# Between the two phases of an attention and mixture-of-experts kernel: the order of the fetches, and which operand the early expert's last block keeps in the array

## The chip, the cores and the metric

One NeuronCore of one Trainium2 chip. The metric is the time of one execution in device microseconds; the time of the kernel before is the median of three runs, 576.55 us (576.1 to 577.07). The profile shows one execution of its own.

## The reference

Linear attention over 8 batches and 8 heads of 576 tokens, with a normalisation, gives 4608 rows of 512 features. Each row is then routed to one of 16 experts (a group of four first, then an expert in it) and goes through that expert's two matrices.

```
kv  = einsum('bhsd,bhse->bhde', k, v)
out = einsum('bhsd,bhde->bhse', q, kv)
x   = out / sqrt(mean(out*out, -1) + 1e-6) * g_norm      # rows of 8*64 = 512
g   = argmax(x @ w_group)                                # 4 groups
e   = argmax(x[rows of g] @ w_expert[g])                 # 4 experts in each
y[rows of g, e] = g_w * e_w * (relu(x @ w1[g, e]) @ w2[g, e])   # 512 -> 1024 -> 512
```

## The kernel before

**Two phases.** The first computes the attention, writes its rows to a table `scr` in HBM, counts the rows of each expert, and, once one expert (the early expert) is known, starts on it: 256 of its rows go through both of its matrices in plain fp32 (`l` in the rows of the profile, lines 299 and 303). What is left of that expert is done at the border: a last quarter of the second layer for these 256 rows (`st["h"]`, `w2c[1]`) and a third block of 128 rows that has yet to be gathered (`xr`, index column `gidx[:, 0, 2:3]`). The second phase is a loop over 15 regions, one expert each, with 364 rows in region 1 down to 256 in the last.

**A region** multiplies in split precision: weights and rows are split in a rounded part and a rest (`whi`, `wlo`, `xh`, `xl`, `hh`, `hl`), and three matmuls stand for one (L310, L311, L315). `split_piece` cuts weights by the piece: a cast on ScalarE (L245) and a subtraction on VectorE (L246). Layer 1 runs over eight feature blocks f, each with 12 matmuls in one of three PSUM buffers `ps`, that ScalarE (`hh`, L284) and then VectorE (`hl`, L285) read out. Layer 2 runs over four blocks in the buffers `psy`.

**Rows for a region** take a long way: an indirect gather from `scr` on GpSimd's queue (`gather`, L252), a scaling (`scale_rows`, L280), a write to HBM (`put_x`, `xd`, L1242), a read back in quarters (`get_x`, `xq`, L1248), a 32x32 transpose on VectorE (`xt`, L1253), and the split (L1262 on ScalarE, L1263 on VectorE).

**What sets the order around the change.** Every engine runs what the program gives it in the order in which the code was written; nothing overtakes on a queue. SyncE (SP) issues the weight loads (`load_half`, L212), `put_x`, `get_x`; GpSimd (POOL) issues gathers (L252) and scatters of finished rows (`scatter_rows`, L256). Weights, their split parts and the early expert's `st["ys"]` (finished rows, `yos`) live in one pool `big` of 12 buffers, used in rotation: a new tile waits until the last reader of its buffer is done, and for `yos` the last readers are two scatters.

At the border, SP's second half load was tied to the gathers by hand:

```
for i in range(2):
    load_next(i, st["gather"] if i else None)
```

and the border's 128 rows kept their rows in the array, so that the result came out by rows and had to be turned:

```
whole1(ps, xT, w1c[hf])        # stationary: 128 rows of xT; moving: 512 columns of weights
nc.scalar.activation(out=hr[:, hf * 512:(hf + 1) * 512], in_=ps, func=AF.Relu)
turn(0); turn(1)               # 8 transposes on TensorE, 2 copies on VectorE
```

The last quarter of the second layer ran in a `psy` buffer, in two parts (`CUT`), with the transposes of `xs` between them; the `psy` buffers were cleared first (L1338). Of the four pieces of region 1's first weights two were split at the border and two in region 1's layer 1 (`w1_at`).

Of the kernel before, what the change touches and what calls it, by code (L numbers as in the profile page):

```python
# [9 lines left out]
F32 = mybir.dt.float32  # L10
# [3 lines left out]
AF = mybir.ActivationFunctionType  # L14
# [40 lines left out]
CUT = 5  # L55

@with_exitstack
def tile_linattn_moe(ctx: ExitStack, tc: tile.TileContext, qm, qt, k, v, router, w1, w2, out):
    nc = tc.nc
    P = 128  # L60
    B, H, S, D = BATCH, HEADS, SEQ, HEAD_DIM
    NTOK, DM = out.shape
# [15 lines left out]
    FC = FF // P  # L78
# [172 lines left out]
    def gather_rows(xg, rows, idx, src=scr):  # L251
        return nc.gpsimd.indirect_dma_start(out=xg[0:rows, 0:RW], out_offset=None, in_=src,  # L252
                                            in_offset=bass.IndirectOffsetOnAxis(ap=idx[0:rows, :], axis=0))

    def scatter_rows(yo, rows, idx):
        sc = nc.gpsimd.indirect_dma_start(  # L256
            out=out, out_offset=bass.IndirectOffsetOnAxis(ap=idx[0:rows, :], axis=0), in_=yo[0:rows, :],
            in_offset=None, bounds_check=NTOK - 1, oob_is_err=False)
        tc.declare_no_dep(sc.ins, group=osc, reason="each token has a row of its own")
        tc.add_to_no_dep_group(osc, sc.ins)  # L260
# [13 lines left out]
    def scale_rows(eng, xg, out_=None):  # L274

        x = by_quarter(xg[:, 0:DM])
        out_ = x if out_ is None else by_chunk(out_)
        for h in range(2):
            hs = slice(2 * h, 2 * h + 2)
            d = eng.tensor_tensor(out=out_[:, hs], in0=x[:, hs], in1=factors(xg)[:, h], op=ALU.mult)  # L280
        return d
# [19 lines left out]
    def whole2(ps, h, w, lo=0, hi=FC):  # L301
        for c in range(lo, hi):
            nc.tensor.matmul(ps, lhsT=h[:, c, :], rhs=w[:, c, :], start=(c == 0), stop=(c == FC - 1))
# [833 lines left out]
    with ExitStack() as ph:  # L1137
# [81 lines left out]
        def next_psy():  # L1219
            psys.append(psys.pop(0))  # L1220
            return psys[-1]
# [8 lines left out]
        def gather(r):  # L1230
            xg = mp.tile([P, 3, RW], F32, name="xg", bufs=1)
            for j, _ in blocks(CAPS[r]):
                st["gather"] = gather_rows(xg[:, j], P, gidx[:, r, j:j + 1])
            return xg
# [5 lines left out]
        def put_x(r, g):  # L1240
            for j, rows in blocks(CAPS[r] + -CAPS[r] % 32):
                nc.sync.dma_start(xd[r % 2][j * P:j * P + rows, :], g[0:rows, j, 0:DM])  # L1242

        def get_x(r):
            n = (CAPS[r] + 31) // 32
            xq = mp.tile([P, 12, P], F32, name="xq", bufs=1)
            for a in range(4):
                nc.sync.dma_start(xq[32 * a:32 * a + 32, 0:n, :], quarter_rows(xd[r % 2], CAPS[r], a))  # L1248
            return xq, mp.tile([P, KC, 384], F32, name="xt", bufs=1)
# [74 lines left out]

        w1c, w2c = st["ws"][0:2], st["ws"][2:4]
        xT = mp.tile([P, KC, P], F32, name="xT", bufs=1)
        hr = mp.tile([P, 12, P], F32, name="hr", tag="yq", bufs=1).rearrange("p c t -> p (c t)")
        xr, xs = (mp.tile([P, 3 * DM], F32, name=nm, tag="yo3")[:, 0:n] for nm, n in (("xr", RW), ("xs", DM)))
        gather_rows(xr, P, gidx[:, 0, 2:3])
        nxt = gather(1)  # L1330
        w1n, w2n, load_next = weight_loads(eidx[0:1, 1:2], mp)
        for i in range(2):
            load_next(i, st["gather"] if i else None)
        scale_rows(nc.vector, xr, xs)
        for j, _ in blocks(CAPS[1]):
            scale_rows(nc.vector, nxt[:, j])
        for x in psys:
            nc.vector.memset(x[:, DM // 2:384], 0.0)  # L1338
        put_x(1, nxt)
        xq, xt = get_x(1)  # L1340
        for i in range(2, 4):
            load_next(i)
        nxt = gather(2)
        scale(2, nxt)
        ps = next_psy()
        o, h1 = ps[:, 0:DM // 2], st["h"]["h"][:, :, P:2 * P]
        whole2(o, h1, w2c[1], hi=CUT)
        tp = ps_t.tile([P, 512], F32, name="tp", tag="pst")
        for c in range(KC):
            nc.tensor.transpose(tp[:, c * P:(c + 1) * P], xs[:, c * P:(c + 1) * P], ident)  # L1350
        nc.scalar.activation(out=xT, in_=tp.rearrange("p (c t) -> p c t", c=KC), func=AF.Copy, scale=g2[:, 0:1])
        whole2(o, h1, w2c[1], lo=CUT)
        nc.scalar.copy(out=st["ys"][:, 1, DM // 2:DM], in_=o)
        for j in range(2):
            scatter_rows(st["ys"][:, j, :], P, gidx0[:, j:j + 1])
        hT = mp.tile([P, FC, 384], F32, name="hT", tag="hl", bufs=1)[:, :, 0:P]

        def turn(hf):
            tp = ps_h.tile([P, 512], F32, name="ps")
            for f in range(4):  # L1360
                nc.tensor.transpose(tp[:, f * P:(f + 1) * P], hr[:, (4 * hf + f) * P:(4 * hf + f + 1) * P], ident)
            nc.vector.tensor_copy(out=hT[:, 4 * hf:4 * hf + 4, :], in_=tp.rearrange("p (f t) -> p f t", f=4))

        for hf in range(2):
            split_piece(w1n, hf)
            ps = ps_h.tile([P, 512], F32, name="ps")
            whole1(ps, xT, w1c[hf])
            nc.scalar.activation(out=hr[:, hf * 512:(hf + 1) * 512], in_=ps, func=AF.Relu)
        turn(0)
        turn(1)  # L1370
        cur = parts_x()
        for c in range(KC):
            turn_x(1, xq, xt, c)
            split_x(1, cur, xt, c)
        yo = mp.tile([P, DM], F32, name="yo", bufs=2)
        for hf in range(2):
            ps = next_psy()
            o = ps[:, 0:DM // 2]
            whole2(o, hT, w2c[hf])
            nc.scalar.copy(out=yo[:, hf * (DM // 2):(hf + 1) * (DM // 2)], in_=o)  # L1380
# [3 lines left out]
        nw1, nw2, load_next = weight_loads(eidx[0:1, 2:3], None)  # L1384
        for i in range(2):
            load_next(i)
        w1_at = {0: 2, 1: 3}
        w2_at = {2: 0, 4: 1, 5: 2, 7: 3}
        todo, results, turns = None, [], iter(())
        tables = overflow_tables()  # L1390
        for r in range(1, NE):
            cap = CAPS[r]
            xh, xl = cur
            hh = mp.tile([P, FC, 384], F32R, name="hh", bufs=1)
            hl = mp.tile([P, FC, 384], F32R, name="hl", tag="hl", bufs=1)
            if nxt:
                xq, xt = get_x(r + 1)
            if todo and todo[0] in MOVED:
                put_y(*todo)
            elif todo:  # L1400
                turns = back(*todo)
            for f in range(FC):
                if f in w1_at:
                    split_piece(w1c, w1_at[f])
                if f in w2_at:
                    split_piece(w2c, w2_at[f], r in MOVED)
                ps = ps_h.tile([P, 512], F32, name="ps")
                layer1(ps[:, 0:cap], w1c, f, xh[:, :, 0:cap], xl[:, :, 0:cap])
                split_h(hh[:, f, 0:cap], hl[:, f, 0:cap], ps[:, 0:cap])
                if r > 1:  # L1410
                    next(tables, None)
                    next(tables, None)
                if f == 0:
                    nxt2 = gather(r + 2) if r + 2 < NE else None
                if nxt2 and f == 1:
                    scale(r + 2, nxt2)
                if f >= 1:
                    next(turns, None)
                if todo and todo[0] in MOVED and f == 2:
                    results = get_y(*todo)  # L1420
                if nxt and f in (1, 3):
                    load_next((f + 3) // 2)
                if nxt2 and f == 4:
                    put_x(r + 2, nxt2)
                if f >= 5 and results:
                    scatter_rows(*results.pop(0))
                if f == FC - 1 and r + 1 == NE:
                    nc.gpsimd.drain()
            nw1a, nw2a, load_a = weight_loads(eidx[0:1, r + 2:r + 3], mp if r % 2 else None) if nxt2 else (None, None, None)
            w1_at, w2_at = {}, {0: 0, 2: 1, 4: 2, 6: 3}  # L1430
            cur = parts_x() if nxt else None

            def side(n, total, after):
                if nxt is None:
                    return
                if not after:
                    split_piece(nw1, n)
                    if n < 2:
                        turn_x(r + 1, xq, xt, 2 * n)
                        turn_x(r + 1, xq, xt, 2 * n + 1)  # L1440
                else:
                    for c in ([0], [1, 2], [3], [])[n]:
                        split_x(r + 1, cur, xt, c)
                    if n in (1, 3) and nxt2:
                        load_a(n // 2)

            if r + 1 == NE:
                layer2_by_token(r, w2c, hh, hl, side)
            else:
                todo = layer2_by_feature(r, w2c, hh, hl, side)  # L1450
            w1c, w2c = nw1, nw2
            nxt, nw1, nw2, load_next = nxt2, nw1a, nw2a, load_a
# [119 lines left out]
```

## Time and profile before

| what | value |
|---|---|
| time, median of 3 runs | 576.55 us (576.1 to 577.07) |
| time of the profiled execution | 575.34 us |
| its span, first to last instruction | 573.6 us |
| TensorE matmul busy | 545.8 us, 95% of the span |
| TensorE weight loads busy | 520.5 us, 91% |
| VectorE / ScalarE / GpSimd busy | 380.0 / 268.5 / 209.7 us |
| chain that ended last | PE 69%, DMA 19%, issue 5% |
| bytes moved by DMA | 164.06 MB, mean 286 GB/s |

The page divides the span into 40 slices; TensorE is busy nine tenths or more in all slices after the first quarter, but for the last. The border lies from about 130 to 180 us from the span's start, and the rows below are from there.

### The profile page before, as it was taken

How to read it: one execution, taken by the hardware profiler on the slowest of the kernel's cores; microseconds unless marked ns; L12 is line 12 of the kernel's file. 1: busy time of each engine (PE TensorE's matmuls, PEld its weight loads, DVE VectorE, ACT ScalarE, POOL GpSimd, SP SyncE). 2: the span in 40 equal slices, each digit the busy share in tenths (PEclk: the TensorE clock that was granted, in tenths of full speed). 3: DMA queues.
4: the chain of work that ended last, by engine and by line, in shares of the span. 5: the costliest groups of instructions: out<-in, count | busy, mean ns of one | idle time of the engine just before them, and what ended most of it. 6: DMA issues, size and time to landing. Idle time of an engine off the chain costs nothing.

```text
span 573.6 us, 11440 instructions
## 1 busy us (share of the span) xinstructions
PE 545.8 (95%) x4287; PEld 520.5 (91%) x4295; DVE 380.0 (66%) x779; ACT 268.5 (47%) x530; POOL 209.7 (37%) x278
## 2 busy tenths in 40 slices
PE   8999978798998999999999999999999999999995
PEld 4789868586688999999999999999999999999995
DVE  4236887772257697676767676777768677887850
ACT  0366754621244445453535454455545455555540
POOL 4015342142265245162426234344425354640221
PEclk9999998899999999999999999999999999999999
DMA  8999999485889999799999999999999999999640
GB/s 269 377 408 380 374 365 403 115 301 151 227 318 315 304 312 325 209 336 244 324 256 333 238 309 259 318 249 318 280 309 253 324 300 337 362 275 287 230 115 34
DMA packets 77360, 164.06 MB, mean 286 GB/s; under 512 B 7980, under 2 KB 46076, under 8 KB 66294
## 3 DMA queue, kind: packets, MB, share of 16 engines
q1 hardware_dynamic: 69331, 141.14, 76.6%
q0 software_dynamic: 7824, 22.11, 12.6%
q8 instruction: 35, 0.57, 0.4%
q10 hardware_dynamic: 146, 0.04, 0.1%
q14 instruction: 24, 0.19, 0.1%
HBM read 125.82 MB, written 37.96 MB: 286 GB/s over the span
## 4 chain that ended last, share of the span: by engine, by line
PE 69%; DMA 19%; issue 5%; DVE 2%; POOL 2%; ACT 1%; SPq 1%; POOLq 0%; DVEq 0%
PE psy L310 10%; PE psy L311 10%; PE psy L315 10%; PE ps L310 10%; PE ps L311 10%; PE ps L315 10%; DMA m_v<-in_v_dram 3%; PE ops L515 3%; DMA m_q<-in_qm_dram 3%; PE l L299 3%; DMA wr<-in_w_dram 2%; DMA m_k<-in_k_dram 2%; PE kps L477 2%; DMA scr<-xo 1%; POOL out_dram L256 1%
## 5 line engine op out<-in xcount | busy, mean ns | idle before, releaser
L246 DVE TENSOR_TENSOR wlo<-wr,whi 128x1024 fp32r<-128x1024 f32 (+1 forms) x172 | 156.7, 936 | 29.9 <-ACT whi L245 23.0
L310 PE MATMUL ps<-xh,whi 128*128 128x364 f32 (+14 forms) x480 | 145.0, 302 | 2.9 <-DVE hl L285 2.4
L311 PE MATMUL ps<-xl,whi 128*128 128x364 f32 (+14 forms) x480 | 144.7, 301 | 0.4 <-DVE xl L1263 0.4
L315 PE MATMUL ps<-xh,wlo 128*128 128x364 f32 (+14 forms) x480 | 144.4, 301 | 0.0
L311 PE MATMUL psy<-hl,whi 128*128 128x364 f32 (+13 forms) x448 | 135.4, 302 | 0.0
L315 PE MATMUL psy<-hh,wlo 128*128 128x364 f32 (+13 forms) x448 | 135.4, 302 | 0.0
L310 PE MATMUL psy<-hh,whi 128*128 128x364 f32 (+13 forms) x448 | 135.3, 302 | 0.0
L245 ACT CAST whi<-wr 128x1024 fp32r<-128x1024 f32 (+1 forms) x172 | 128.2, 783 | 0.0
L284 ACT ACTIVATE hh<-ps 128x364 fp32r<-128x364 f32 (+14 forms) x120 | 50.4, 420 | 150.2 <-PE ps L315 149.0
L310 PEld LDWEIGHTS ps<-xh,whi 128*128 128x128 f32 x480 | 90.8, 189 | 3.6 <-DVE hl L285 2.7
L256 POOL DMA_INDIRECT out_dram<-yo,gall x45 | 51.2, 1137 | 113.1 <-DMA yo<-yd 95.4
L311 PEld LDWEIGHTS ps<-xl,whi 128*128 128x128 f32 x480 | 90.5, 189 | 0.9 <-DVE xl L1263 0.9
L285 DVE SCALAR_TENSOR_TENSOR hl<-ps,hh 128x364 fp32r<-128x364 f32 (+14 forms) x120 | 55.8, 465 | 52.9 <-ACT hh L284 52.9
L315 PEld LDWEIGHTS ps<-xh,wlo 128*128 128x128 f32 x480 | 90.7, 189 | 0.0
L280 POOL TENSOR_TENSOR xg<-xg 128x256 f32<-128x256 f32 x82 | 63.0, 794 | 69.6 <-DMA xg<-scr,gall 69.6
L310 PEld LDWEIGHTS psy<-hh,whi 128*128 128x128 f32 x448 | 84.7, 189 | 0.0
L315 PEld LDWEIGHTS psy<-hh,wlo 128*128 128x128 f32 x448 | 84.7, 189 | 0.0
L311 PEld LDWEIGHTS psy<-hl,whi 128*128 128x128 f32 x448 | 84.5, 189 | 0.0
L252 POOL DMA_INDIRECT xg<-scr,gall x44 | 50.0, 1136 | 83.0 <-DMA xd<-xg 73.3
L1262 ACT ACTIVATE xh<-xt,rw 128x364 fp32r<-128x364 f32 (+14 forms) x60 | 32.6, 544 | 48.6 <-DVE xt L1253 48.6
L1315 DVE STREAM_TRANSPOSE yq<-psy 128x320 f32<-128x320 f32 (+3 forms) x52 | 26.7, 513 | 29.6 <-PE psy L315 29.5
L515 PE MATMUL ops<-kvx,m_q 128*128 128x168 f32 x256 | 42.0, 312 | 1.3 <-ACT xr L466 0.6
(257 smaller groups left out, 592.6 us busy)
## 6 DMA issues: line engine op xcount, KB each, us to landing
wr<-in_w_dram SPq DMA_DIRECT2D x64, 1024.0 KB, 9.2
scr<-xo SPq DMA_DIRECT2D x36, 256.0 KB, 8.9
m_q<-in_qm_dram SPq DMA_DIRECT2D x8, 1024.0 KB
xd<-xg SPq DMA_DIRECT2D x32, 256.0 KB, 6.7
m_k<-in_k_dram SPq DMA_DIRECT2D x7, 1024.0 KB, 8.3
m_v<-in_v_dram SPq DMA_DIRECT2D x7, 1024.0 KB
yo<-yd SPq DMA_DIRECT2D x26, 256.0 KB, 4.0
xq<-xd SPq DMA_DIRECT2D x20, 160.0 KB, 10.2
```

Of the source, the lines that this page charges most:

```text
L245: nc.scalar.copy(out=hi, in_=x)
L246: nc.vector.tensor_tensor(out=lo, in0=x, in1=hi.bitcast(F32), op=ALU.subtract)
L252: return nc.gpsimd.indirect_dma_start(out=xg[0:rows, 0:RW], out_offset=None, in_=src, in_offset=bass.IndirectOffsetOnAxis(ap=idx[0:rows, : ...
L256: sc = nc.gpsimd.indirect_dma_start(out=out, out_offset=bass.IndirectOffsetOnAxis(ap=idx[0:rows, :], axis=0), in_=yo[0:rows, :], in_offset ...
L280: d = eng.tensor_tensor(out=out_[:, hs], in0=x[:, hs], in1=factors(xg)[:, h], op=ALU.mult)
L284: nc.scalar.activation(out=hh, in_=ps, func=AF.Relu)
L285: nc.vector.scalar_tensor_tensor(out=hl, in0=ps, scalar=0.0, in1=hh.bitcast(F32), op0=ALU.max, op1=ALU.subtract)
L310: nc.tensor.matmul(ps, lhsT=stat_h(c), rhs=mov_h(c), start=(c == 0), stop=False)
L311: nc.tensor.matmul(ps, lhsT=stat_h(c), rhs=mov_l(c), start=False, stop=False)
L315: nc.tensor.matmul(ps, lhsT=stat_l(d), rhs=mov_h(d), start=False, stop=(d == n - 1))
L515: nc.tensor.matmul(o, lhsT=raw["q", b].rearrange("p j f -> p (j f)")[:, (pr * NJ + j) * P:(pr * NJ + j + 1) * P], rhs=kvx[b % 4][:, pr], s ...
L1262: nc.scalar.activation(out=xh, in_=x, func=AF.Copy, scale=g2[:, 0:1])
```

## The change

The order of the border's steps is rewritten, and the early expert's third block keeps weights in the array instead of rows:

- SP: both half loads of region 1's first weights are issued at once, with no tie to the gathers.
- POOL: the three gathers of region 1 come first, that of `xr` after them; the scatter of the first half of `yos` is issued right behind, that of the second after region 2's rows have been scaled.
- DVE: region 1's rows are scaled first, `xr` last; each is written to `xd` when it is scaled. The clearing of `psy` moves into region 1's layer 1.
- PE: the last quarter of layer 2 goes to a buffer `left` of the pool `ps_t` in one piece; layer 1 of the third block becomes 32 matmuls of 128 moving columns, with weights stationary, instead of 8 of 512; the 8 transposes and 2 copies of `turn` are gone.
- All four pieces of region 1's first weights are split at the border, before the rows `xt` are turned and split; region 1's second weights are then split at the same places as in the other regions.

```diff
-        hr = mp.tile([P, 12, P], F32, name="hr", tag="yq", bufs=1).rearrange("p c t -> p (c t)")
+        hT = mp.tile([P, 12, P], F32, name="hT", tag="yq", bufs=1)[:, 0:FC]
...
-        gather_rows(xr, P, gidx[:, 0, 2:3])
-        nxt = gather(1)
         w1n, w2n, load_next = weight_loads(eidx[0:1, 1:2], mp)
         for i in range(2):
-            load_next(i, st["gather"] if i else None)
-        scale_rows(nc.vector, xr, xs)
+            load_next(i)
+        nxt = gather(1)
+        gather_rows(xr, P, gidx[:, 0, 2:3])
+        scatter_rows(st["ys"][:, 0, :], P, gidx0[:, 0:1])
         for j, _ in blocks(CAPS[1]):
             scale_rows(nc.vector, nxt[:, j])
-        for x in psys:
-            nc.vector.memset(x[:, DM // 2:384], 0.0)
         put_x(1, nxt)
+        scale_rows(nc.vector, xr, xs)
...
-        ps = next_psy()
-        o, h1 = ps[:, 0:DM // 2], st["h"]["h"][:, :, P:2 * P]
-        whole2(o, h1, w2c[1], hi=CUT)
+        left = ps_t.tile([P, 512], F32, name="left", tag="pst")
+        whole2(left[:, 0:DM // 2], st["h"]["h"][:, :, P:2 * P], w2c[1])
+        nc.scalar.copy(out=st["ys"][:, 1, DM // 2:DM], in_=left[:, 0:DM // 2])
...
-        whole2(o, h1, w2c[1], lo=CUT)
-        nc.scalar.copy(out=st["ys"][:, 1, DM // 2:DM], in_=o)
-        for j in range(2):
-            scatter_rows(st["ys"][:, j, :], P, gidx0[:, j:j + 1])
...
+        scatter_rows(st["ys"][:, 1, :], P, gidx0[:, 1:2])
...
-        for hf in range(2):
-            split_piece(w1n, hf)
-            ps = ps_h.tile([P, 512], F32, name="ps")
-            whole1(ps, xT, w1c[hf])
-            nc.scalar.activation(out=hr[:, hf * 512:(hf + 1) * 512], in_=ps, func=AF.Relu)
-        turn(0)
-        turn(1)
+        for hf in range(2):
+            ps = ps_h.tile([P, 512], F32, name="ps")
+            for f in range(4):
+                whole1(ps[:, f * P:(f + 1) * P], w1c[hf][:, :, f * P:(f + 1) * P], xT)
+            nc.scalar.activation(out=hT[:, 4 * hf:4 * hf + 4], in_=ps.rearrange("p (f t) -> p f t", f=4), func=AF.Relu)
+            for p in range(2 * hf, 2 * hf + 2):
+                split_piece(w1n, p)
...
-        w1_at = {0: 2, 1: 3}
-        w2_at = {2: 0, 4: 1, 5: 2, 7: 3}
+        w2_at = {0: 0, 2: 1, 4: 2, 6: 3}
```

How the instructions stand is shown at three places. First TensorE at the border, from the last full early product `l` to region 1's first matmul (`xs` are the third block's rows, `xT` the same turned, `hr` and `hT` its hidden layer by rows and by features). Before:

```order
L303 MATMUL l_1912<-wr_1673,h 128x256 x8
L303 MATMUL psy_1942<-wr_1708,h 128x256 x5
L1350 MATMUL tp<-ident,xs 128x128 x4
L303 MATMUL psy_1942<-wr_1708,h 128x256 x3
L299 MATMUL ps<-wr_1539,xT 128x512 x4
L299 MATMUL ps<-wr_1576,xT 128x512 x4
L1361 MATMUL ps<-ident,hr 128x128 x8
L303 MATMUL psy_1943<-wr_1673,hT 128x256 x8
L303 MATMUL psy_1944<-wr_1708,hT 128x256 x8
L310 MATMUL ps<-xh,whi 128x364
```

and with the change:

```order
L303 MATMUL l_1912<-wr_1673,h 128x256 x8
L303 MATMUL left<-wr_1708,h 128x256 x8
L1349 MATMUL tp<-ident,xs 128x128 x4
L299 MATMUL ps<-xT,wr_1539 128x128 x16
L299 MATMUL ps<-xT,wr_1576 128x128 x16
L303 MATMUL ps<-wr_1673,hT 128x256 x8
L303 MATMUL ps<-wr_1708,hT 128x256 x8
L310 MATMUL ps<-xh,whi 128x364
```

Eight matmuls of `left` now stand together ahead of the transposes of `xs`; the 8 matmuls of 512 columns became 32 of 128, and the turning of `hr` is gone.

Second, VectorE from the split of region 1's rows into its layer 1, with the semaphores that each row waits for (DMAHW are counters of SP's DMAs, DMASW of those on POOL's queue). Before (`wr_1961` is the second half of the first weights, `wr_1983` the first half of the second):

```order
L1263 SCALAR_TENSOR_TENSOR xl<-xt,rw,xh 128x364 [waits Activation_49]
L246 TENSOR_TENSOR wlo<-wr_1961,whi 128x4x256 [waits DMAHW5_49,Activation_49]
L285 SCALAR_TENSOR_TENSOR hl<-ps,hh 128x364 [waits Activation_49]
L246 TENSOR_TENSOR wlo<-wr_1961,whi 128x4x256 [waits Activation_49]
L285 SCALAR_TENSOR_TENSOR hl<-ps,hh 128x364 [waits Activation_49]
L246 TENSOR_TENSOR wlo<-wr_1983,whi 128x16x32 [waits DMASW7_49,DMAHW5_49,DMASW0_49,Activation_49]
L246 TENSOR_TENSOR wlo<-wr_1983,whi 128x16x32 [waits Activation_49]
L285 SCALAR_TENSOR_TENSOR hl<-ps,hh 128x364 [waits Activation_49] x2
```

and with the change, from the last two pieces of the first weights (`wr_1956` is their second half):

```order
L246 TENSOR_TENSOR wlo<-wr_1956,whi 128x4x256 [waits DMAHW5_49,Activation_49]
L246 TENSOR_TENSOR wlo<-wr_1956,whi 128x4x256 [waits Activation_49]
L1253 STREAM_TRANSPOSE xt<-xq 128x384 [waits DMAHW3_49,DMAHW4_49,DMAHW2_49,DMAHW1_49]
L1263 SCALAR_TENSOR_TENSOR xl<-xt,rw,xh 128x364 [waits Activation_49]
...
L246 TENSOR_TENSOR wlo<-wr_1983,whi 128x16x32 [waits DMAHW5_49,PE_49,Activation_49]
L246 TENSOR_TENSOR wlo<-wr_1983,whi 128x16x32 [waits Activation_49]
L285 SCALAR_TENSOR_TENSOR hl<-ps,hh 128x364 [waits Activation_49]
L1400 MEMSET psy_1942 128x128
L285 SCALAR_TENSOR_TENSOR hl<-ps,hh 128x364 [waits Activation_49]
```

Two subtractions moved ahead of the first transpose `xt`, and the first subtraction of the second weights waits for TensorE where it waited for POOL's two DMAs.

Third, SP where it loads the first weights of region 2's expert (`wr_2091` and `wr_2093` before, `wr_2108` and `wr_2110` now), between the writes `xd` of region 2's rows and their read-back `xq`:

```order
-L212 DMA wr_2091<-in_w_dram 128x2048 [waits DMAHW2_49]
-L212 ISA
-L212 DMA wr_2093<-in_w_dram 128x2048 [waits DMAHW3_49]
+L1242 DMA xd_58<-xg 128x512 [waits DMASW6_49,Pool_49]
+L1242 DMA xd_58<-xg 128x512 [waits DMAHW1_49,DMASW7_49,Pool_49]
+L207 TENSOR_LOAD eidx
+L212 ISA
+L212 DMA wr_2108<-in_w_dram 128x2048 [waits DMAHW2_49,PE_49,Activation_49]
+L212 ISA
+L212 DMA wr_2110<-in_w_dram 128x2048 [waits DMASW4_49,DMAHW3_49,DMASW0_49,Activation_49]
 L1248 DMA xq<-xd_58 32x12x128 [waits DMAHW4_49,DMAHW1_49,DMAHW7_49,DMAHW0_49,DVE_49]
```

The waits for POOL's two scatters have moved here: the second half of that load takes the buffer of `yos`, and region 2's read-back stands behind it.

## Rows read from the trace of the kernel before

**Rows 1.** The page, busy time by engine over the whole span.
```profile
PE 545.8 (95%) x4287; PEld 520.5 (91%) x4295; DVE 380.0 (66%) x779; ACT 268.5 (47%) x530; POOL 209.7 (37%) x278
```

**Rows 2.** The chain that ended last, 128 to 180 us: start, us, what.
```profile
143.96 6.77 DMA xd<-xg
...
152.14 6.41 DMA xq<-xd
158.67 0.59 DVE xt L1253
...
166.99 7.96 DMA out_dram<-yos,gall
175.03 0.17 DVE wlo L246
...
176.24 0.54 DVE hl L285
```

**Rows 3.** Timeline of PE at the border: start, us, line, operation, [idle before <-releaser].
```profile
133.21 7.15 PE L303 MATMUL l<-wr,h 128*128 128x256 f32 x32
143.22 2.43 PE L303 MATMUL psy<-wr,h 128*128 128x256 f32 x10 [2.86 <-DVE psy L1338]
145.48 0.60 PE L1350 MATMUL tp<-ident,xs 128*128 128x128 f32 x4
...
147.22 7.03 PE L299 MATMUL ps<-wr,xT 128*128 128x512 f32 x16
...
155.47 7.17 PE L303 MATMUL psy<-wr,hT 128*128 128x256 f32 x32
...
166.27 0.33 PE L310 MATMUL ps<-xh,whi 128*128 128x364 f32 x1
```

**Rows 4.** Timeline of PE later in region 1, and region 2's first matmul.
```profile
174.13 0.33 PE L315 MATMUL ps<-xh,wlo 128*128 128x364 f32 x1
176.82 0.43 PE L310 MATMUL ps<-xh,whi 128*128 128x364 f32 x1 [2.36 <-DVE hl L285]
...
198.99 0.32 PE L310 MATMUL ps<-xh,whi 128*128 128x354 f32 x1
```

**Rows 5.** Weight loads: timeline of the first phase, and those of one line (duration ns min/median/max).
```profile
62.98 1.15 PEld L515 LDWEIGHTS ops<-kvx,m_q 128*128 128x128 f32 x8 [0.24 <-issue]
...
94.65 1.00 PEld L497 LDWEIGHTS eps__1463<-gw,kvt 128*128 128x128 f32 x8
...
L299 PEld LDWEIGHTS ps<-wr,xT x16: 190/190/190, 147.0 to 153.2; 128*128 128x128 f32 x16
```

**Rows 6.** Timeline of DVE at the border and in region 1's layer 2.
```profile
142.21 0.76 DVE L280 TENSOR_TENSOR xg<-xg 128x256 f32<-128x256 f32 x2 [0.79 <-DMA xg<-scr,gall]
...
152.41 1.23 DVE L246 TENSOR_TENSOR wlo<-wr,whi 128x1024 fp32r<-128x1024 f32 x1 [2.42 <-ACT whi L245]
...
185.73 1.03 DVE L1253 STREAM_TRANSPOSE xt<-xq 128x384 f32<-128x384 f32 x2
...
195.68 0.55 DVE L1263 SCALAR_TENSOR_TENSOR xl<-xt,rw,xh 128x354 fp32r<-128x354 f32 x1
```

**Rows 7.** Timeline of ACT at the border.
```profile
146.25 0.69 ACT L1351 ACTIVATE xT<-tp,rw 128x512 f32<-128x512 f32 x1 [5.48 <-PE tp L1350]
147.42 0.37 ACT L1353 COPY yos<-psy 128x256 f32<-128x256 f32 x1 [0.48 <-PE psy L303]
...
151.34 1.04 ACT L245 CAST whi<-wr 128x1024 fp32r<-128x1024 f32 x1
154.28 0.60 ACT L1368 ACTIVATE hr<-ps 128x512 f32<-128x512 f32 x1 [1.90 <-PE ps L299]
```

**Rows 8.** Timeline of SP's queue: start of the first issue, us to the end of the last.
```profile
130.56 11.99 SPq L212 DMA_DIRECT2D wr<-in_w_dram  x2
...
167.51 5.97 SPq L1248 DMA_DIRECT2D xq<-xd  x4
```

**Rows 9.** Windows of 2 us: PE, PEld, DVE, ACT, POOL busy, PEclk, DMA share, GB/s.
```profile
132.00:134.00 2.00, 2.00 (x12) 1.68 (x11) 0.21 (x1) 0.37 (x1) 0.00 (x0) 1.00 0.90 352
```

More of the change, by code (lines that the diff above doesn't have):

```diff
@@ L1351, in tile_linattn_moe @@
         nc.scalar.activation(out=xT, in_=tp.rearrange("p (c t) -> p c t", c=KC), func=AF.Copy, scale=g2[:, 0:1])
-        whole2(o, h1, w2c[1], lo=CUT)
-        nc.scalar.copy(out=st["ys"][:, 1, DM // 2:DM], in_=o)
-        for j in range(2):
-            scatter_rows(st["ys"][:, j, :], P, gidx0[:, j:j + 1])
-        hT = mp.tile([P, FC, 384], F32, name="hT", tag="hl", bufs=1)[:, :, 0:P]
-        def turn(hf):
-            tp = ps_h.tile([P, 512], F32, name="ps")
-            for f in range(4):
-                nc.tensor.transpose(tp[:, f * P:(f + 1) * P], hr[:, (4 * hf + f) * P:(4 * hf + f + 1) * P], ident)
-            nc.vector.tensor_copy(out=hT[:, 4 * hf:4 * hf + 4, :], in_=tp.rearrange("p (f t) -> p f t", f=4))
-        for hf in range(2):
-            split_piece(w1n, hf)
-            ps = ps_h.tile([P, 512], F32, name="ps")
-            whole1(ps, xT, w1c[hf])
-            nc.scalar.activation(out=hr[:, hf * 512:(hf + 1) * 512], in_=ps, func=AF.Relu)
-        turn(0)
-        turn(1)
+        scatter_rows(st["ys"][:, 1, :], P, gidx0[:, 1:2])
+        for hf in range(2):
+            ps = ps_h.tile([P, 512], F32, name="ps")
+            for f in range(4):
+                whole1(ps[:, f * P:(f + 1) * P], w1c[hf][:, :, f * P:(f + 1) * P], xT)
+            nc.scalar.activation(out=hT[:, 4 * hf:4 * hf + 4], in_=ps.rearrange("p (f t) -> p f t", f=4), func=AF.Relu)
+            for p in range(2 * hf, 2 * hf + 2):
+                split_piece(w1n, p)
         cur = parts_x()
@@ L1376, in tile_linattn_moe @@
         for hf in range(2):
-            ps = next_psy()
+            ps = ps_h.tile([P, 512], F32, name="ps")
             o = ps[:, 0:DM // 2]
@@ L1402, in tile_linattn_moe @@
             for f in range(FC):
-                if f in w1_at:
-                    split_piece(w1c, w1_at[f])
                 if f in w2_at:
@@ L1412, in tile_linattn_moe @@
                     next(tables, None)
+                elif f < len(psys):
+                    nc.vector.memset(psys[f][:, DM // 2:384], 0.0)
                 if f == 0:
@@ L1429, in tile_linattn_moe @@
             nw1a, nw2a, load_a = weight_loads(eidx[0:1, r + 2:r + 3], mp if r % 2 else None) if nxt2 else (None, None, None)
-            w1_at, w2_at = {}, {0: 0, 2: 1, 4: 2, 6: 3}
             cur = parts_x() if nxt else None
```

## The prediction, made before the changed kernel ran

> **What bounds the kernel now.** I read the page first: TensorE is busy 95% of the span [rows 1], so time can only be won where it stands still or does dispensable work. The waits by engine come next, and they put TensorE's idle time after the first phase into this border; from region 2 on no wait of any length is left on it. Then the chain that ended last, and the timelines of the engines at the border.
>
> The reader should see two losses. **First**, region 1 starts late. TensorE ends the early products at 133.21 + 7.15 = 140.4, idles 2.86 us until VectorE has cleared `psy`, and comes to region 1 behind the third block's work [rows 3]; there it waits piecemeal for region 1's rows. I measure that by the start of layer 1's second feature block (f = 1), at 166.27 [rows 3]. The chain says why: the write `xd` takes 6.77 us, the read-back 6.41, and the first transpose starts only at 158.67 [rows 2]. From it to f = 1 are 166.27 - 158.67 = 7.6 us.
>
> **Second**, a stall inside region 1: f = 5 should follow the row at 174.13, but starts at 176.82, after 2.36 us of idle [rows 4]. The profile names `hl`, and the chain shows what held it: the scatters of `yos`, 7.96 us from 166.99, then the subtraction `wlo` at 175.03, then `hl`, then TensorE [rows 2]. The subtraction writes into a buffer that those scatters still read; VectorE runs in order, so `hl` stood behind it and TensorE had no free `ps`. The price: from 166.27 to 174.13 are 47 matmul starts, 0.1672 us each. The 180 matmuls of f = 1 to the end of layer 2 should then take 30.1 us, to 196.37; region 2 starts at 198.99 [rows 4]. **The stall costs 2.6 us.**
>
> **The change, step by step.**
>
> *Leftover quarter.* `left` has a PSUM buffer of its own and no wait, so its 8 matmuls start at 140.3. Sixteen matmul records of this shape take half of 7.17 us [rows 3]: 3.6, to 143.9. The rows `xs` that come next are now fourth in the gathers. The fourth gather's rows were scaled at 142.21 + 0.76 = 142.97 [rows 6], 0.9 us before they are needed: hidden, as long as the gathers are no slower. The memsets, now in layer 1 of region 1, lie in VectorE's idle time there.
>
> *Transposes and `xT`.* Before, 147.22 - 145.48 = 1.74 us passed from the transposes to layer 1, covered by other matmuls [rows 3]. Now nothing covers them. The four transposes take 0.60 us [rows 3], to 144.5; the copy of `left`, 0.37 us [rows 7], is ahead on ScalarE and done as they end; `xT` takes 0.69 us [rows 7]. With hand-overs layer 1 starts at 145.4, not 147.22.
>
> *Layer 1 with stationary weights.* 32 matmuls of two passes each are 64 weight loads, where there were 16 under 512 columns. No row has 128 fp32 columns. With 40 columns, where the load can be all that counts, eight loads take 1.00 us, the last whole: (1.00 - 0.19)/7 = 0.116 us apart; with 168 columns (1.15 - 0.19)/7 = 0.137 [rows 5]. 128 lies between, and its streaming alone, a quarter of the 512 columns' 7.03/16 [rows 3], is 0.110, so I take 0.118, near the lower row: 7.6 us, between 7.4 and 8.8. Layer 1 ends at 153.0; layer 2 started at 155.47 before, after 8.25 us of layer 1 and turning. So TensorE gains another 0.6 us here.
> The Trainium skill, "TensorE: Matmul & The Clock Gate", section "LDWEIGHTS (loading the stationary operand)", gives a load as its columns over 1.2 GHz, 107 ns for 128. By that estimate the sum would be 0.7 us better; the rows' 116 ns stand here.
>
> *Splitting ahead of the rows.* The last two pieces of the first weights now sit between layer 1 and the transposes `xt`: on ScalarE behind the relu of the second half. Relu 0.60 us from 153.1, two casts of 1.04 [rows 7], to 155.8, and the last subtraction, 1.23 [rows 6]: `xt` starts at 157.05. This is the new path; TensorE, done with layer 2 of the block at about 160, waits for it. With the same 7.6 us behind, f = 1 starts at 164.65. **Gain 1.6 us.** What the two pieces freed at f = 0 and 1 was covered there.
>
> *Rows of region 1.* They must be back by 157.05. SP no longer sits 11.99 us at the second weight load [rows 8], and region 1's gathers move one place ahead: the third write `xd` goes out at about 141.6 instead of 143.96 [rows 2]. With the write and the read-back as slow as before the rows are back at 158.67 - 2.4 = 156.3; hidden, though by little. They should be quicker, since no megabyte of weights goes just ahead of the write.
>
> *The buffer of `yos`.* VectorE's row in region 1 waits for no POOL counter any more; SP's second half load for region 2 does, 1 MB wanted only in the second half of region 1's layer 2. **Gain 2.6 us.** Behind it on SP stand the read-back `xq` of region 2 and the second weights of its expert.
>
> **Sum.** 1.6 + 2.6 = 4.2 us. The profiled execution took 575.34 us over a span of 573.6, so it would take 571.1; its time is 1.2 us under the median, against which the same gain gives 576.55 - 4.2 = **572.3 us**.
>
> **The rivals.**
>
> *Thin matmuls don't hide their loads.* If each load's whole 0.190 us [rows 5] were paid, layer 1 takes 12.2 us, 4.6 more; f = 1 is at 169.25, 3.0 late, and with 2.6 won the time is 576.9: no change. For it: the moving side shrinks to a quarter, and every load is longer than 128 columns stream. Against it: loads of this shape run 0.116 us apart, overlapping [rows 5]. [...]
>
> *The gathers pay for the weights.* The second megabyte now moves while they do. One took 352 GB/s in the window where it was alone [rows 9], 3.0 us. If the gathers lost all of that, `xs` is ready at 146.0, 2.1 us late: gain 2.1, 574.4. Against it: the gathers are spaced by their issue, and the last is issued some 3 us after that load should be through. The Trainium skill, "DMA: Bandwidth & Descriptors", section "Queues, rings and completion order", has each DMA engine take turns between queues; by that the gathers share, not stop; no row here shows it alone.
>
> *The stall stays*, because the second weights' parts wait for something else as late: 576.55 - 1.6 = 574.95.
>
> *Slower: SP stands still for the scatter.* POOL issues the second `yos` scatter only after region 2's rows are gathered and scaled; SP's half load waits for it, and region 2's read-back behind that. If the scatter lands as late as before, at 174.95 [rows 2], the read-back goes out 7.4 us after 167.51 [rows 8], and its transposes start at 193.1 instead of 185.73. From them to the last split are 195.68 + 0.55 - 185.73 = 10.5 us [rows 6]; region 2 needs that 1.5 us after its start, so it starts at 202.1, 3.1 later than before: 579.7. With region 2 forecast at 198.99 - 4.2 = 194.8, it costs from a start of those transposes at 194.8 + 1.5 - 10.5 = 185.8 on, and makes the change slower from 190.0. Against it: the row writes, gathers and scatters all start several microseconds earlier, and `xq`'s buffer is free only with the fourth `xt`, near 163, anyhow.
>
> **How the numbers follow.** My forecast 0.72; the gathers 0.10; the stall stays 0.05; thin matmuls 0.07; SP's wait 0.06. Within the forecast, 7.0 to 8.8 us for layer 1 moves the time by -0.6 to +1.2, and the runs before spread by half a microsecond either way: 571.0 to 574.1. With the rival at 574.4 the range is **571.0 to 574.7**. A difference of 0.2%, 1.15 us, is about what a measurement of this kernel tells from none. Faster 0.87 (forecast, gathers, stall stays), within it 0.07, slower 0.06.
>
> **What would show it.** Right: no idle before `left`; 64 loads about 0.118 us apart; `xt` starting right behind the fourth `wlo`, near 157; f = 1 near 164.6; no idle of TensorE from there on, and region 2 starting near 194.8. Wrong: transposes `xs` that wait for a gather; `xt` that waits for `xq`; loads 0.19 apart; a wait of VectorE for `xq` at the start of region 1's layer 2.

## The result, and the profile after

| | before | with the change |
|---|---|---|
| time, median | 576.81 us (4 runs, 576.1 to 578.22) | 571.98 us (4 runs, 569.92 to 573.12) |
| ratio | | 0.9891, 95% interval 0.9858 to 0.9923 |
| profiled execution | 575.34 us | 569.92 us |
| its span | 573.6 us | 568.2 us |

The change is faster, as forecast. The ratio makes 6.3 us of the 576.55 (4.4 to 8.2), so 570.3 us, where 4.2 us and 572.3 were forecast: the gain was put too small, and the time by the ratio lies 0.7 us under the low end of the range. (The two medians of the table are 4.8 us apart; the ratio on record, 6.3 us, is the figure used below, and 4.8 lies within its interval.) Repeated with eight runs beside 23 of before, the ratio was the same (0.9891, 0.9857 to 0.9926).

The page's busy line first, beside [rows 1]: TensorE works as long as before in a span that is 5.4 us shorter.

```profile
PE 545.6 (96%) x4335; PEld 523.7 (92%) x4335; DVE 376.8 (66%) x777; ACT 268.5 (47%) x530; POOL 208.9 (37%) x278
```

The timeline of PE at the border and the first matmul of region 2 (start, us, line, operation, idle before and what ended it), against [rows 3, 4]:

```profile
132.81 7.15 PE L303 MATMUL l<-wr,h 128*128 128x256 f32 x32
139.80 3.62 PE L303 MATMUL left<-wr,h 128*128 128x256 f32 x16
143.25 0.60 PE L1349 MATMUL tp<-ident,xs 128*128 128x128 f32 x4
144.95 7.41 PE L299 MATMUL ps<-xT,wr 128*128 128x128 f32 x64 [1.10 <-ACT xT L1350]
152.20 7.07 PE L303 MATMUL ps<-wr,hT 128*128 128x256 f32 x32
...
161.00 0.43 PE L310 MATMUL ps<-xh,whi 128*128 128x364 f32 x1 [0.52 <-ACT xh L1262]
...
162.75 0.43 PE L310 MATMUL ps<-xh,whi 128*128 128x364 f32 x1 [0.51 <-ACT xh L1262]
...
163.82 0.33 PE L310 MATMUL ps<-xh,whi 128*128 128x364 f32 x1
...
193.91 0.32 PE L310 MATMUL ps<-xh,whi 128*128 128x354 f32 x1
```

The reader should see that no wait stands ahead of `left`, that 64 records of thin matmuls fill 7.25 us (to the row at 152.20), and that the only waits left are for `xT` and, piecemeal, for region 1's rows. The first phase ended 0.40 us sooner in this execution than in that of before (132.81 against 133.21), in code that is the same, so from here on times count from **the start of the last 32 records of early products**, and I call it the mark. f = 1 starts 31.01 us after the mark (before 33.06), region 2 61.10 (before 65.78). From f = 1 to region 2 are 30.09 us, without a stall.

The chain that ended last, as in [rows 2]; only the longer pieces:

```profile
141.05 3.17 DMA xd<-xg
...
144.95 7.43 PE ps L299 x64
152.40 0.60 ACT hT L1357
153.00 0.94 ACT whi L245
153.97 0.98 DVE wlo L246
155.11 1.22 DVE wlo L246
156.32 0.50 DVE xt L1253
```

The write `xd` takes 3.17 us where it took 6.77, the read-back `xq` is no longer on the chain, and the first transpose `xt` comes right behind the fourth `wlo`: the path that the prediction named. (That `xd` still stands here says little: the profile names it for the 0.39 us that ScalarE waits ahead of `xT`, and in e8 below puts the same 0.39 us down to the transposes `tp`.) SP's queue, against [rows 8], shows the price that it named as well, a half load that waits for the second scatter of `yos`:

```profile
130.16 0.90 SPq L212 DMA_DIRECT2D wr<-in_w_dram  x2
...
144.55 1.89 SPq L1248 DMA_DIRECT2D xq<-xd  x4
...
160.26 6.43 SPq L212 DMA_DIRECT2D wr<-in_w_dram  x2
166.87 2.24 SPq L1248 DMA_DIRECT2D xq<-xd  x4
```

### The profile page after: what moved, and what is told of

The parts are those of the page before. It is cut to its first block, busy times and chain, and to the rows that moved or that the text cites. A ratio compares the mean times of both kernels' runs of the same rounds, so it can differ in the third digit from the quotient of the medians.

```text
span 568.2 us, 11528 instructions
## 1 busy us (share of the span) xinstructions
PE 545.6 (96%) x4335; PEld 523.7 (92%) x4335; DVE 376.8 (66%) x777; ACT 268.5 (47%) x530; POOL 208.9 (37%) x278
## 4 chain that ended last, share of the span: by engine, by line
PE 77%; DMA 13%; issue 3%; DVE 2%; ACT 2%; POOL 1%; SPq 1%; POOLq 0%; DVEq 0%; ACTq 0%
PE psy L310 11%; PE psy L315 11%; PE psy L311 11%; PE ps L311 11%; PE ps L315 11%; PE ps L310 11%; DMA m_v<-in_v_dram 3%; DMA m_q<-in_qm_dram 3%; PE l L299 3%; DMA m_k<-in_k_dram 3%; PE ops L515 2%; DMA scr<-xo 2%; PE kps L477 2%; PE ps L299 1%; DMA xs<-scr,sidx 1%
## 5 line engine op out<-in xcount | busy, mean ns | idle before, releaser
L256 POOL DMA_INDIRECT out_dram<-yo,gall x45 | 55.5, 1234 | 110.9 <-DMA yo<-yd 90.4
L280 POOL TENSOR_TENSOR xg<-xg 128x256 f32<-128x256 f32 x82 | 61.1, 770 | 80.4 <-DMA xg<-scr,gall 80.4
L252 POOL DMA_INDIRECT xg<-scr,gall x44 | 47.5, 1079 | 76.1 <-DMA xd<-xg 60.8
```

The source lines that it names most:

```text
L256: sc = nc.gpsimd.indirect_dma_start(out=out, out_offset=bass.IndirectOffsetOnAxis(ap=idx[0:rows, :], axis=0), in_=yo[0:rows, :], in_offset ...
```

## The experiments

The traces explained 4.7 us at the border, and 0.7 more in code that no line of the change touches. Two things were open: which part of the change brings what, and whether the gain of 6.3 us has a share that these two traces don't show. All kernels in one table, from their traces and timed runs (f = 1 and region 2 in us after the mark; the last column is from region 2's start to the end of the span):

| kernel | f = 1 | region 2 | ratio to before (95%) | rest |
|---|---|---|---|---|
| before, first trace | 33.06 | 65.78 | | 374.59 |
| before, three more traces | 32.72, 32.87, 32.71 | 66.87, 67.32, 66.93 | | 374.52, 374.40, 374.38 |
| changed, first trace | 31.01 | 61.10 | 0.9891 (0.9858 to 0.9923) | 374.26 |
| e1, changed again | 31.05 | 61.14 | 0.9891 (0.9857 to 0.9926) | 374.42 |
| e2, before with the splits alone | 32.89 | 62.99 | 0.9939 (0.9908 to 0.9970) | 374.45 |
| e3, changed, rows in the array | 31.15 | 61.10 | 0.9883 (0.9844 to 0.9922) | 372.76 |
| e4, changed, late splits | 28.31 | 63.18 | 0.9914 (0.9884 to 0.9945) | 373.99 |
| e5, changed, early splits | 28.46 | 58.55 | 0.9823 (0.9788 to 0.9858) | 374.43 |
| e6, e5 with rows in the array | 29.94 | 59.87 | 0.9851 (0.9811 to 0.9892) | 372.77 |
| e7, e5 with `left` cut | 28.95 | 59.04 | 0.9838 (0.9803 to 0.9872) | 374.26 |
| e8, changed, SP tied again | 34.76 | 68.15 | 0.9990 (0.9961 to 1.0019) | 375.29 |
| e9, splits behind `xs`, `left` cut | 28.01 | 58.10 | 0.9833 (0.9785 to 0.9882) | 374.43 |

**e1: the changed kernel again.** No edit.

> The changed kernel once more, nothing edited, in more rounds. Theory A, from the two traces: between the last early products and region 2's start 4.7 us were won (2.05 at the border, 2.63 by the stall that is gone), and 0.7 us more of the traces' difference lies in code that is the same in both; so a gain of 4.7 us, a ratio near 0.992. Theory B: the first comparison's middle, 0.9891, is the true size, and a third part of some 1.5 us lies outside the border, in places that the traces would show again; a gain of 6.3 us. A middle above 5.5 us speaks for B, below it for A.

The border came out the same to 0.04 us, and the ratio too: 6.3 us (4.3 to 8.2). By the middle that is B; but the trace shows no third place, since the rest after region 2 differs by 0.17 us from before. So the missing 1.6 us had to be sought in before's other executions (below, b1 to b3).

**e2: the splits alone.** In the kernel before, two pieces move from region 1 to the border:

```diff
         turn(1)
+        for p in range(2, 4):
+            split_piece(w1n, p)
...
-        w1_at = {0: 2, 1: 3}
-        w2_at = {2: 0, 4: 1, 5: 2, 7: 3}
+        w1_at, w2_at = {}, {0: 0, 2: 1, 4: 2, 6: 3}
```

> The kernel before, with one part of the change alone: all four pieces of region 1's first weights are split at the border (two of them behind the copies of the turned hidden layer), and region 1's second weights at f = 0, 2, 4, 6. Theory A (the stall in region 1 is VectorE's wait for the buffer of yos, and the order of the splits alone takes it away): region 1's rows are back no sooner, so f = 1 stays near 166.3; no stall; region 2 starts 2.6 us earlier, near 196.4; time 2.6 us under before. Theory B (the stall goes only if the scatters of yos are issued earlier as well): the wait shows up elsewhere on VectorE or SP, region 2 starts near 199, time as before.

A: f = 1 stays (32.89), the stall goes, and region 2 starts 2.79 us sooner than in the first trace of before (forecast 2.6). That part of the change needs none of the others: what counts is whose buffer the first subtraction of region 1 takes, as e4 shows from the other side.

**e3: rows in the array again.** In the changed kernel:

```diff
-            for f in range(4):
-                whole1(ps[:, f * P:(f + 1) * P], w1c[hf][:, :, f * P:(f + 1) * P], xT)
-            nc.scalar.activation(out=hT[:, 4 * hf:4 * hf + 4], in_=ps.rearrange("p (f t) -> p f t", f=4), func=AF.Relu)
+            whole1(ps, xT, w1c[hf])
+            nc.scalar.activation(out=hr[:, hf * 512:(hf + 1) * 512], in_=ps, func=AF.Relu)
+            if hf:
+                turn(0)
+                turn(1)
```

> The changed kernel, but the third block keeps rows in the array again: 16 matmuls of 512 columns with 8 transposes and 2 copies of the turned hidden layer, ahead of the last two pieces' splits. Theory A (the splits and not TensorE set region 1's start): the copies put the last subtractions back by some 0.4 us, f = 1 goes from 163.8 to 164.2 or 164.5, TensorE's extra 2.4 us of work fill its waits; time 0.3 to 0.7 us over the changed kernel. Theory B (TensorE's own work at the border counts in full): 2.4 us over it.

A, and more plainly than expected: f = 1 0.14 us later, region 2 at 61.10 in both (its matmuls from f = 1 on took 29.95 us for 30.09, see the last section). TensorE's shorter work fell into its own wait for the rows. The operand that gives the change half its name is worth nothing to region 1's start as long as the splits bind it.

**e4: late splits.** In the changed kernel the pieces go back to where they were split before (two ahead of layer 1's halves, two at f = 0 and 1, `w1_at` and `w2_at` as before).

> The changed kernel, but with the pieces split as before: two ahead of the two halves of layer 1, two at f = 0 and 1 of region 1, the second weights at f = 2, 4, 5, 7. Theory A (the chain ended with the splits): the first transpose xt starts with the rows' arrival, at 152.5 or sooner, and f = 1 near 161.0 instead of 163.8; but the first subtraction in region 1 then takes the buffer of yos and must wait for the second scatter, which landed near 166.2 in the changed kernel; VectorE stands, hl of f = 0 comes at about 168, TensorE runs out of ps buffers near 165 and idles 2 to 3 us; time as the changed kernel or up to 1.5 us above. Theory B (the early fetches did it, the order of the splits is indifferent): 2.5 to 2.8 us under the changed kernel, no stall.

A: f = 1 comes 2.7 us sooner, and region 1 gives it back and 2.1 us more. VectorE's timeline, and TensorE's:

```profile
169.29 1.22 DVE L246 TENSOR_TENSOR wlo<-wr,whi 128x1024 fp32r<-128x1024 f32 x1 [6.71 <-DMA out_dram<-yos,gall]
170.43 0.53 DVE L285 SCALAR_TENSOR_TENSOR hl<-ps,hh 128x364 fp32r<-128x364 f32 x1
```
```profile
171.01 0.43 PE L310 MATMUL ps<-xh,whi 128*128 128x364 f32 x1 [2.98 <-DVE hl L285]
```

The subtraction stood 6.71 us for the scatter of `yos`, `hl` behind it, TensorE behind `hl`: the stall of [rows 4] in another place. (In the window from 170 to 180 the clock was 0.83 as well.) So the four pieces at the border are not there to be early for TensorE; they shift the rotation of the buffers.

**e8: SP tied again.** In the changed kernel, the second half load waits for the last gather as it did before:

```diff
-            load_next(i)
-        nxt = gather(1)
+            load_next(i, st["gather"] if i else None)
```
(with `nxt = gather(1)` ahead of the loads).

> The changed kernel, but SP's second half load of region 1's first weights waits for the last gather again, so that 1 MB goes ahead of the row writes. Theory A (the splits bound region 1, the rows have some 3.5 us of slack): the write of rows takes near 6.8 us instead of 3.2, xt starts within 0.6 us of before the edit, f = 1 at 31.0 to 31.6 us from the last early products, region 2 at 61.1 to 61.7. Theory B (the early fetch is what the border gained): f = 1 at 33.0 as in the kernel before, region 2 at 63.1.

Neither: it is worse than B. The chain of e8 shows both transfers of the rows:

```profile
144.08 9.70 DMA xd<-xg
...
155.19 5.59 DMA xq<-xd
```

The write took 9.70 us behind the megabyte, not 6.8. The first `xt` waited for the read-back and started 26.37 us after the mark, 2.9 later than in the changed kernel, and f = 1 came 3.75 us later. Region 2 came 7.05 later; of the other 3.3 us some 0.9 are a wait for `hl`, and most of the rest is neither a wait nor more work. Windows of e8 (PE, PEld, DVE, ACT, POOL busy, **PEclk**, DMA share, GB/s) and rows of PE show it:

```profile
164.00:169.00 5.00, 4.23 (x9) 2.17 (x10) 3.12 (x5) 2.77 (x6) 3.17 (x5) 0.51 0.71 279
169.00:174.20 5.20, 5.20 (x19) 5.20 (x19) 0.00 (x0) 1.51 (x4) 3.98 (x5) 0.50 0.92 285
```
```profile
169.28 0.51 PE L310 MATMUL ps<-xh,whi 128*128 128x364 f32 x1
169.59 0.51 PE L311 MATMUL ps<-xl,whi 128*128 128x364 f32 x1
```

TensorE had waited in pieces for region 1's rows; then its granted clock stood at 0.5, the 1.2 GHz level, for 10 us, and a matmul of 364 columns came every 0.30 us, where it comes every 0.167 at full clock: the 16 behind f = 1's start took 4.86 us for 2.67. This was in no theory. The Trainium skill, "TensorE: Matmul & The Clock Gate", section "What's actually happening", has the lower level follow upon too little activity; the trace agrees.

**b1 to b3: the kernel before, three more traces.** If waits at the border can halve the clock there, they may do so in the kernel before, whose own waits are 2.86 and 2.36 us long [rows 3, 4], though its first trace shows none of it.

> The kernel before once more, unedited, for another trace of it. Theory A (the waits at its border let TensorE's clock fall in some executions, which the first trace does not show, and the changed kernel is spared that): where the mean granted clock is below 0.987, a stretch at half clock lies between 140 and 190 us, matmuls of 364 columns take 0.51 us instead of 0.33 there, and region 2 starts more than 66.5 us after the last early products, not 65.8. Theory B (all that varies lies in the first phase and the tail, alike in both kernels): region 2 at 65.8 whatever the clock.

> As the run before it, the kernel before for another trace: theory A, with a clock below 0.987 a stretch at half clock between 140 and 190 us and region 2 later than 66.5 us after the last early products; theory B, 65.8.

> As the two runs before it: theory A, with a clock below 0.987 a stretch at half clock between 140 and 190 us and region 2 later than 66.5 us after the last early products; theory B, 65.8.

A for two, and the mechanism for all three: region 2 starts 66.87, 67.32 and 66.93 us after the mark, and each has a stretch at half clock in region 1 (b1's mean clock was 0.989, so the bound of 0.987 was mine and wrong). Of b2, the windows (PE busy, PEclk, DMA share, GB/s) and the rows of PE behind the two waits:

```profile
144.00:147.50 3.50, 2.98 (x7) 0.51 0.85 225
147.50:150.00 2.50, 2.50 (x15) 1.00 0.93 315
...
178.00:181.60 3.60, 3.47 (x11) 0.53 1.10 196
181.60:184.00 2.40, 2.40 (x16) 1.00 1.19 205
```
```profile
144.52 3.86 PE L303 MATMUL psy<-wr,h 128*128 128x256 f32 x10 [2.87 <-DVE psy L1338]
...
178.13 0.65 PE L310 MATMUL ps<-xh,whi 128*128 128x364 f32 x1 [2.57 <-DVE hl L285]
178.57 0.51 PE L311 MATMUL ps<-xl,whi 128*128 128x364 f32 x1
...
181.77 0.33 PE L310 MATMUL ps<-xh,whi 128*128 128x364 f32 x1
```

The first stretch makes ten records take 3.86 us for the 2.43 of [rows 3], but f = 1 is no later (32.87): the wait for `xq` behind it swallows that. The second lies behind the stall, and nothing swallows it: from 178.13 to 181.60 eleven matmuls took 3.47 us, at full clock 11 x 0.167 = 1.84. The same window of the first trace of before, then of b1 and of b3 (PE busy, PEclk, DMA share, GB/s):

```profile
170.00:180.00 10.00, 7.64 (x46) 1.00 1.06 339
170.00:180.00 10.00, 7.47 (x38) 0.83 1.06 302
170.00:180.00 10.00, 7.68 (x38) 0.85 1.06 327
```

Of the four traces of before the first alone has its clock whole in region 1; in both traces of the changed kernel it is whole from the mark to the end of region 2 and on. The window view of the changed kernel, across the place where f = 1 to 7 run:

```profile
164.00:178.00 14.00, 14.00 (x85) 1.00 0.99 272
```

**e5, e6, e7, e9: a better version.** e5 splits the four pieces where ScalarE and VectorE still idle:

```diff
         scatter_rows(st["ys"][:, 0, :], P, gidx0[:, 0:1])
+        for p in range(2):
+            split_piece(w1n, p)
...
         scale_rows(nc.vector, xr, xs)
+        for p in range(2, 4):
+            split_piece(w1n, p)
         xq, xt = get_x(1)
...
-            for p in range(2 * hf, 2 * hf + 2):
-                split_piece(w1n, p)
```

> The changed kernel, but the four pieces are split where ScalarE and VectorE still idle: two right behind the gathers' issue, two behind the scaling of xs, all ahead of the third block. Counted from the start of the last 32 records of early products, the changed kernel has f = 1 at 31.0 us and region 2 at 61.1 us; with late splits f = 1 stood at 28.1, then a stall. Theory A (the subtractions ahead of xt are what region 1 waits for, and their place sets the buffer of yos): f = 1 at 28.1 as there, no stall, region 2 at 58.2, time 2.9 us under the changed kernel. Theory B (the rows' read-back xq becomes the bound): f = 1 between 28.5 and 31, with xt waiting for xq.

A: f = 1 at 28.46, no stall, region 2 2.55 us sooner than with the change; 0.9823 to before. VectorE's first `xt` does wait for `xq`, as B has it, but early enough: TensorE now comes to region 1 with no wait for its rows. e6 puts e3's edit on top of it:

> The same with early splits, but rows stationary in the third block, with the 8 transposes and 2 copies. With late subtractions the operand made no difference to region 2's start (61.10 us in both). Theory A (TensorE's own work is the path once the splits are out of the way): layer 1 and turning take 8.4 us where the stationary weights take 7.25, so f = 1 is 1.1 us later than with early splits and stationary weights, near 29.2, and region 2 near 59.3. Theory B (the operand is worth nothing here either): 58.2.

A: f = 1 1.48 and region 2 1.32 us later than e5. Only now, with the splits out of the way, does the operand count at region 2's start. (Its timed runs don't tell it from e5, and its rest after region 2 is 1.66 us shorter; see the last section.) e7 cuts `left` behind its fifth matmul, transposes `xs` between the parts, and copies `left` behind `xT`:

> Early splits, and the last quarter left in two parts again, with the transposes of xs between them and its copy behind xT. The 1.10 us that TensorE waits for xT are then filled by the second part, if xs is there in time (it is scaled 0.4 us before left ends in the changed kernel). Theory A (nothing but TensorE's own work is left): f = 1 and region 2 about 1.0 us earlier than with early splits alone, near 27.1 and 57.2. Theory B: the transposes wait for xs by what they start sooner, some 0.7 us, or region 1 then waits for xq; no more than 0.3 us won.

B: the transposes wait 1.81 us for `xs`, and region 2 is 0.5 us later than e5's. GpSimd's timeline in e7, third and fourth gather:

```profile
138.87 1.58 POOL L252 DMA_INDIRECT xg<-scr,gall  x1 [0.30 <-issue]
140.75 1.17 POOL L252 DMA_INDIRECT xr<-scr,gall  x1 [0.31 <-issue]
```

Their issue took 1.58 and 1.17 us, in the changed kernel 0.95 each; VectorE's subtractions ran from 138.40 to 140.76, so beside the third, and its scaling from 140.68 on, so beside the fourth. e9 moves all four pieces behind the scaling of `xs` and cuts `left` behind its seventh matmul:

> The changed kernel with all four pieces split right behind the scaling of xs, so that VectorE is idle while GpSimd issues the gathers, and with the last quarter cut behind its seventh matmul, the transposes of xs between. Theory A (a gather's issue grew from 0.95 to 1.2 to 1.6 us because VectorE's subtraction ran beside it, and that made xs late): each gather's issue stays at 0.95 to 1.06 us, xs is scaled 10.1 us from the start of the last early products (10.7 and 11.0 with early splits), layer 1 starts at 11.6 where it was 12.3, f = 1 at 27.8 and region 2 at 57.9. Theory B (the gathers are late for the transfers' sake): issue as long as there, xs at 10.5 or later, region 2 at 58.5.

A: region 2 at 58.10, the earliest of all, and the same two gathers, then the first two of region 2:

```profile
136.16 0.95 POOL L252 DMA_INDIRECT xg<-scr,gall  x1 [0.30 <-issue]
137.41 0.95 POOL L252 DMA_INDIRECT xr<-scr,gall  x1 [0.30 <-issue]
...
145.31 1.47 POOL L252 DMA_INDIRECT xg<-scr,gall  x1 [5.62 <-DVE wlo L246]
147.08 0.95 POOL L252 DMA_INDIRECT xg<-scr,gall  x1 [0.30 <-issue]
```

The subtractions now run from 142.44 to 147.06: the long issue moved with them, to 145.31. By its runs e9 (0.9833) can't be told from e5 (0.9823); either beats the kernel before, near 567 us against 576.55. Against the changed kernel the traces give e5 2.6 and e9 3.0 us to region 2's start, while the intervals of the ratios touch or overlap.

## Where the prediction was right, and where it fell short

Each step, in us after the mark (133.21 in the trace that it was made from):

| step | forecast | measured |
|---|---|---|
| layer 1 of the third block starts | 145.4 - 133.21 = 12.2 | 12.14 |
| its 64 loads | 64 x 0.118 = 7.6 | 7.25, or 0.113 each |
| region 1's rows back | 156.3 - 133.21 = 23.1 | 19.9 and 20.5 (e4, e5, where `xt` waits for them) |
| first `xt` | 157.05 - 133.21 = 23.8 | 156.24 - 132.81 = 23.4 |
| f = 1 | 164.65 - 133.21 = 31.4 | 31.01 |
| f = 1 to region 2 | 30.1 | 30.09 |
| region 2 | 194.8 - 133.21 = 61.6 | 61.10 |

**The steps held.** `left` starts without a wait; `xs` is ready at 142.89, 0.36 us before `left` ends (0.9 was forecast); the splits take the read-back's place on the path; the stall is worth 2.6 to 2.8 us (e2). Up to f = 1 the gain is 2.05 us, where 1.6 was forecast. The loads were mis-sized by 0.35 us: 0.113 us apart, under the lower of the two rows that I bounded them by. The 107 ns that the Trainium skill, "TensorE: Matmul & The Clock Gate", section "LDWEIGHTS (loading the stationary operand)", gives is about as far off on the other side. Against the execution that the sum was made from, 571.1 us was forecast and 569.92 measured; the 1.2 us are 0.5 at the border, 0.4 in the first phase and 0.3 behind region 2.

**What failed is the price of the stall, and with it the step from that execution to the median**: "its time is 1.2 us under the median, against which the same gain gives 576.55 - 4.2". I took the 1.2 us for scatter that stays. By the traces it was in good part the clock's answer to the very waits that the change takes away. The term "the stall costs 2.6 us" holds for an execution whose clock stays whole; where the clock fell behind the stall, before's region 2 started 67.0 us after the mark on average (66.87, 67.32, 66.93) and not 65.78. Over all four traces of before it is 66.7, over the two of the changed kernel 61.1: 5.6 us at the border and 0.1 behind it, where 4.2 were forecast and 6.3 (4.3 to 8.2) timed. Of the 1.5 us between 4.2 and 5.7, 0.9 is this term, 0.5 the terms of the border and 0.1 lies behind it; the border alone would have left the time at 571.9, inside the range. The 0.6 us between 5.7 and 6.3 stay open. They are within the interval, but e5 too is timed at 10.2 us (8.2 to 12.2) where the traces give 8.2, so before's other executions may lose more than its four traces show; no run here settles it. The sign of it was there: the waits of [rows 3, 4] are the longest on TensorE behind the first phase, and a mean clock of 0.992 was that of one execution; I had no other, and put no term and no range for it. (The range is also a little off by its own terms: 572.3 less 0.6 and 0.5 is 571.2, not 571.0.)

**The rivals.** Thin matmuls that pay whole loads: the 64 loads are 0.113 apart, not 0.19. Gathers that pay for the second megabyte: the first three gathers were issued 1.3 to 1.4 us apart, as before, while the window of [rows 9], 132 to 134, moved 410 GB/s, not 352, and the next, 134 to 136, 442; `xs` was late for nobody. The stall that stays: gone. SP standing for the scatter: it does stand, for most of the 6.43 us that its row of two loads lasts, but the second scatter is issued at 159.47, so region 2's read-back goes out at 166.87; region 2's first transpose starts at 180.66 and waits for nothing.

**What each part is worth** the prediction had only in part. The operand: 1.0 us of TensorE's own time (8.25 - 7.25, where it said 0.6), but 0.14 us of f = 1 and 0.00 of region 2's start (e3). Counted to the end of the span, with the shorter rest of e3 and e6, the kernels with rows in the array are not behind at all: e3 is 1.5 us ahead of the changed kernel, e6 0.3 ahead of e5. So no run here shows that this half of the change makes the whole kernel faster. The splits at the border: 2.8 us (e2). The early fetches: the prediction had the rows "hidden, though by little", and quicker perhaps; they are back about 3 us sooner than it put them. With SP tied again the changed kernel is as slow as the kernel before (e8, 0.999): 3.75 us up to f = 1, 2.9 of them because the rows come later, and 3.3 behind it, 2.2 of them by the clock.

## What to carry to other kernels

A wait on TensorE can have two prices: its length, and the work behind it at half clock, which one trace may not show (here 1.1 to 1.5 us of region 2's start, behind a stall of 2.3 to 2.6); before the gain of a removed wait is summed, look at the granted clock of several executions, not of one. A step that seems to be moved for its own sake may be there for the rotation of buffers: compare what each instruction waits for. And where a faster operand falls into another engine's wait it brings nothing until that wait is gone: take the splits away from the path first. Even then count it to the end of the kernel, not to the next stage.

## What had not been expected

- **The half-clock stretches at the border.** By the windows some 3.5 us behind one stall (b2), some 10 us behind a row of waits (e8). Of the five traces with a wait of over 2 us in region 1's layer 1 (the four of before, e4), four have one behind it; e8 has one though none of TensorE's waits there is longer than 1.17 us; the other eight traces have none. The wait for `psy`, 2.70 to 2.91 us in the four traces of before and in e2, has one behind it in two of the five (b2, b3). So a wait of this length may or may not bring one; what decides it is not shown.
- **VectorE slows GpSimd's gathers.** With a subtraction beside it a gather's issue took 1.33 to 1.58 us (e5, e6, e7, and e9 in region 2), with a scaling beside it 1.17 (e7), instead of 0.95 (e9). The Trainium skill, "SBUF — State Buffer", section "SBUF: two separate sides", says that a VectorE operation with two SBUF inputs and a GpSimd operation that reads SBUF exclude each other; the traces agree.
- **The same matmuls at another pace.** e3 and e6, the two kernels with rows in the array and the change's other edits, took 372.8 us from region 2 to the end, all other traces 374.0 to 375.3, at full clock and with no line edited there: the 192 matmuls of 302 columns took 26.59 us in both, 26.74 in the others. It shows already in region 1, where f = 1 to region 2 took 29.95 and 29.93 us for 30.09. One thing in the code sets the two apart: they take six of the rotating `ps` buffers at the border, all other kernels four, so that with three in rotation region 1 starts on another buffer. Whether that is the cause was not tried.
